# First h from raw x, DMA transposes and 3.5-chunk q and S in a fused linear-attention and gated-MLP kernel

## The chip, the cores and the metric

The kernel runs on one NeuronCore of a Trainium2 chip. Times are device microseconds (us) of whole executions. A single profiled execution of each kernel gives the span, the engines' busy times and the waits; the span is 1.7 to 2.3 us shorter than the time of the same run. PE is TensorE's matmul stream, PEld its weight loads, DVE VectorE, ACT ScalarE, POOL GpSimd, and SP the engine whose queue issues nearly all DMAs ("SPq" in the profile). PSUM is the memory that TensorE writes; the kernel uses eight parts of it, called banks.

## The reference

Token count 2048, width 448 (3.5 times 128), hidden width 1792, 16 heads of 28. All arrays are bfloat16.

```python
xn = layernorm(x)                       # over the last axis, eps 1e-5
q, k, v = split_heads(xn @ wqkv)        # linear attention: no softmax
pq, pk = phi(q), phi(k)                 # where(t > 0, t + 1, exp(t)) + 1e-6
kv, z = sum_s pk[s] v[s], sum_s pk[s]
o = (pq @ kv) / (pq @ z + 1e-6)
s = o @ wo
h = relu(xn @ w1 + b1) ** 2             # 1792 columns
g = silu(h @ w2 + b2)
return x + s * g
```

## The kernel before

All work is recorded as operations with estimated durations. PE and SP run them in the order in which they are written; a small list scheduler chooses the order on DVE, ACT and POOL from those estimates, and the order is then fixed. Tokens come in 16 tiles of 128, handled as four groups of four tiles.

```python
def pe_transpose(tiles):                 # xn -> xT, on PE, through one PSUM bank
    ... last = e.transpose(v[:, o : o + P], xn[:, si, c * P : (c + 1) * P], ident[:, :])
    ... # evicted (copied out of PSUM) by DVE (0.69 us for two tiles) or ACT

def pe_four(a, b, c, d):                 # four output tiles, all matmuls on 64 rows;
    ...                                  # the two halves of the array run side by side
for g in range(NG):                      # groups of four token tiles
    if g == 0:
        pe_transpose([1]); pe_two(kk(0), kk(1), False)
        pe_transpose([2, 3]); pe_two(kk(2), kk(3), True)
    if g + 1 < NG:
        ln(4 * g + 4, 4 * g + 8)         # statistics, rstd, normalise, copy of columns 384..447
    ...                                  # K, q and h of this group, in groups of four
    pe_transpose([4 * g + 4, 4 * g + 5])
    pe_transpose([4 * g + 6, 4 * g + 7])
    ...
# then token sums (xn^T pk), folds (these sums times the v weights, then times wo), den (pq @ z),
# spreads (1/den repeated over a head's columns), gate tiles gg(si) = h[si] @ w2 and S tiles ss(si)
```

The width of 448 leaves a half chunk of 64 rows. The kernel before copies columns 384 to 447 of xn a second time, so that the transposed half chunk lies on both halves of the partitions, and runs h, K and q in 64-row halves that pack without loss. q and S use four chunks of 112 columns (four heads each). A "gate tile" below is 14 matmuls of 448 columns; h is 14 output tiles a group.

## Time and profile before

158.31 us median of two runs (157.43 and 159.19); span of the profile 157.6 us.

| what | value | where it is read |
|---|---|---|
| PE busy | 148.4 of 157.6 us | page, busy times |
| useful PE work begins, h begins, PE ends | 7.5, 14.6, 153.7 us | timeline |
| tail after PE's last matmul | 3.9 us | timeline |
| transposes on PE | 16 matmuls in about 1.0 us, four groups | timeline |

The page of the kernel before: busy times with their share of the span, then the span in 40 equal slices, where 9 means busy at least 90% and PEclk is the clock granted to TensorE in tenths.

```profile
PE 148.4 (94%) x1131; PEld 76.5 (49%) x1131; DVE 105.9 (67%) x237; ACT 70.8 (45%) x129; POOL 35.4 (22%) x49
PE   5969999999999869999999999999999999999990
PEclk9999999999999987999999999999999999999999
```

PE is the bound, with small dents in slices 2 and 13 to 14 (counted from 0). After the second dent the clock is lower (8 and 7). The waits of PE, kernel before: engine and line that waited, what released it, us in total, times, longest.

```profile
PE pb L463 <- DVE xn L449: 2.2, 2, 1.9
PE pb L564 <- DVE xT L473: 0.8, 1, 0.8
```

The timeline of PE around that dent, kernel before: start, us, engine, line, operation, tiles, shapes, count, and in brackets the idle time before it.

```profile
52.37 1.03 PE L597 MATMUL pb<-xT,w 64*128 64x512 bf16 x8
...
56.63 1.07 PE L463 MATMUL pb<-ident,xn 128*128 128x128 bf16 x16 [1.94 <-DVE xn L449]
57.63 1.70 PE L585 MATMUL pb<-xT,w_qkv 64*112 64x512 bf16 x8
59.12 1.91 PE L597 MATMUL pb<-xT,w 64*128 64x512 bf16 x8
```

Eight h matmuls take 1.03 us at 52.4 us and 1.91 us at 59.1 us: after 1.94 us of waiting and 1.0 us of transposes the clock was halved for about 3.4 us. This happens in some executions only: of 40 runs of this kernel taken later, those with a mean granted clock of 0.984 to 0.988 took 158.8 to 160.0 us, those with 0.994 to 1.0 took 157.2 to 158.2. The 1.6 us between them is what this stretch costs.

### The profile page before, as it was taken

To read this page: it belongs to the slowest core of one execution; us is meant where nothing else is said; L and a number is where in the kernel's file an instruction comes from. 1 tells how busy PE (TensorE), PEld (TensorE's weight loads), DVE (VectorE), ACT (ScalarE), POOL (GpSimd) and SP (SyncE) were. 2 spreads that over 40 slices of the span, in tenths; PEclk is the share of its full clock that TensorE was granted. 3 is DMA by queue.
4 is the path that set the end of the run, shared out by engine and by line. 5 is a ranking of instruction groups with operands and counts; after the bars stand their busy time and mean duration, and the time that the engine had idled before them with its cause. 6 is when DMAs were issued, how large, how long until landed. Compare 5 with 4: busy or idle time off the path is not lost.

```text
span 157.6 us, 2827 instructions
## 1 busy us (share of the span) xinstructions
PE 148.4 (94%) x1131; PEld 76.5 (49%) x1131; DVE 105.9 (67%) x237; ACT 70.8 (45%) x129; POOL 35.4 (22%) x49
## 2 busy tenths in 40 slices
PE   5969999999999869999999999999999999999990
PEld 5834545455444444445454454444555555555540
DVE  0879896789995992969998056799633444433373
ACT  3442688768787752877811269512211112211110
POOL 7502500055001630007300000000022522233252
PEclk9999999999999987999999999999999999999999
DMA  4999991000000000000000000000001110001013
GB/s 130 324 402 296 347 294 38 0 2 0 4 0 0 4 0 0 0 4 0 2 0 4 0 0 2 4 0 0 0 0 50 41 58 29 29 29 33 29 55 120
DMA packets 7721, 9.19 MB, mean 58 GB/s; under 512 B 604, under 2 KB 6812, under 8 KB 7708
## 3 DMA queue, kind: packets, MB, share of 16 engines
q1 hardware_dynamic: 7148, 8.55, 17.7%
q10 hardware_dynamic: 560, 0.46, 0.9%
q8 instruction: 9, 0.15, 0.4%
q14 instruction: 4, 0.03, 0.1%
HBM read 7.17 MB, written 1.84 MB: 57 GB/s over the span
## 4 chain that ended last, share of the span: by engine, by line
PE 86%; DVE 6%; DMA 3%; SPq 2%; ACT 1%; issue 0%; DVEq 0%
PE pb L755 27%; PE pb L597 25%; PE pb L783 8%; PE pb L585 7%; PE pb L564 6%; PE pb L626 6%; DMA b1r<-in_B_b_dram 3%; PE pb L463 3%; DVE xn L421 2%; SPq L365 2%; DVE pk L554 1%; PE pb L632 1%; DVE pk L547 1%; PE pb L734 1%; DVE xT L473 1%; DVE xn L449 1%
## 5 line engine op out<-in xcount | busy, mean ns | idle before, releaser
L597 PE MATMUL pb<-xT,w 64*128 64x512 bf16 x392 | 48.2, 381 | 0.0
L755 PE MATMUL pb<-w,r 128*128 128x448 bf16 x224 | 44.9, 353 | 0.0
L606 ACT ACTIVATE r<-pb,b1f 128x512 bf16<-128x512 f32 x56 | 34.9, 691 | 8.3 <-PE pb L597 8.3
L755 PEld LDWEIGHTS pb<-w,r 128*128 128x128 bf16 x224 | 21.6, 98 | 20.7 <-issue 0.9
L597 PEld LDWEIGHTS pb<-xT,w 64*128 64x128 bf16 x392 | 19.0, 95 | 22.6 <-issue 1.4
L797 POOL TENSOR_TENSOR obuf<-obuf,x_tok 128x448 bf16<-128x448 bf16 x14 | 14.3, 1032 | 63.9 <-DVE obuf L792 63.9
L772 ACT ACTIVATE gbuf<-gbuf 128x448 bf16<-128x448 bf16 x16 | 9.2, 577 | 41.9 <-DVE gbuf L764 41.9
L764 DVE TENSOR_TENSOR gbuf<-pb,b2b 128x448 bf16<-128x448 f32 x16 | 10.0, 625 | 23.5 <-PE pb L755 23.1
L612 DVE TENSOR_TENSOR r<-r 128x512 bf16<-128x512 bf16 x56 | 20.6, 433 | 7.5 <-ACT r L606 7.5
L575 POOL TENSOR_TENSOR zacc<-zacc,pk 128x448 f32<-128x448 f32 x13 | 13.7, 1055 | 46.8 <-DVE pk L554 45.4
L585 PE MATMUL pb<-xT,w_qkv 64*112 64x512 bf16 x112 | 15.7, 395 | 0.0
L564 PE MATMUL pb<-w_qkv,xT 64*128 64x448 bf16 (+1 forms) x100 | 12.8, 350 | 1.3 <-DVE xT L473 0.8
L783 PE MATMUL pb<-msb,pqT 112*128 112x448 bf16 x64 | 13.9, 352 | 0.0
L542 ACT ACTIVATE pqT<-pb 112x512 bf16<-112x512 f32 x16 | 8.7, 594 | 10.3 <-PE pb L585 10.3
L401 DVE BATCH_NORM_STATS2 st<-x_tok 128x6 f32<-128x448 bf16 x16 | 9.4, 613 | 4.3 <-DMA x_tok<-in_A_x_dram 4.3
L792 DVE TENSOR_TENSOR obuf<-pb,gbuf 128x448 bf16<-128x448 f32 x16 | 10.0, 625 | 2.1
L554 DVE SCALAR_TENSOR_TENSOR pqT<-pb,pqT 112x512 bf16<-112x512 f32 x16 | 10.9, 688 | 0.3
L585 PEld LDWEIGHTS pb<-xT,w_qkv 64*112 64x112 bf16 x112 | 7.5, 133 | 5.9 <-issue 1.3
L542 ACT ACTIVATE pk<-pb 128x448 bf16<-128x448 f32 x16 | 7.8, 540 | 5.1 <-PE pb L564 5.1
L547 DVE TENSOR_SCALAR pk<-pk 128x448 bf16<-128x448 bf16 x16 | 6.8, 432 | 4.6 <-ACT pk L542 4.6
L742 DVE TENSOR_TENSOR pqT<-pqT,pb 112x512 bf16<-112x512 bf16 x16 | 9.9, 680 | 0.0
L554 DVE SCALAR_TENSOR_TENSOR pk<-pb,pk 128x448 bf16<-128x448 f32 x16 | 9.6, 619 | 0.3
(60 smaller groups left out, 100.8 us busy)
## 6 DMA issues: line engine op xcount, KB each, us to landing
out_dram<-obuf SPq DMA_DIRECT2D x16, 112.0 KB, 1.7
w<-in_B_w_dram SPq DMA_DIRECT2D x1, 1568.0 KB, 16.2
x_tok<-in_A_x_dram SPq DMA_DIRECT2D x3, 448.0 KB, 9.4
w<-in_B_w_dram SPq DMA_DIRECT2D x1, 1344.0 KB, 8.2
w_qkv<-in_A_wqkv_dram SPq DMA_DIRECT2D x2, 336.0 KB, 7.9
x_tok<-in_A_x_dram SPq DMA_DIRECT2D x2, 224.0 KB, 3.7
w<-in_B_w_dram SPq DMA_DIRECT2D x2, 224.0 KB, 8.9
w_o<-in_A_wo_dram SPq DMA_DIRECT2D x1, 392.0 KB, 17.3
```

The source lines that it names most:

```text
L542: "act", lambda e, _: e.activation(out=slot, in_=ps(buf)[0:rows, 0:n], func=AF.Exp), [buf, "actw"],
L554: lambda e, _: e.scalar_tensor_tensor(out=slot, in0=ps(buf)[0:rows, 0:n], scalar=1.0 + 1e-6, in1=slot, op0=ALU.add, op1=ALU.max),
L564: return e.matmul(ps(b)[:, 0:D], xT[rows, c, si * P : (si + 1) * P], w_qkv[rows, c, D : 2 * D], start=start, stop=stop)
L575: lambda e, _: e.tensor_tensor(out=o[:, :], in0=pk[:, 0, :] if i == 1 else zacc[:, :], in1=pk[:, i, :], op=ALU.add),
L585: return e.matmul(ps(b)[0:PD, 0:512], w_qkv[rows, c, m * PD : (m + 1) * PD], xT[rows, c, g * 512 : (g + 1) * 512], start=start, stop=stop,)
L597: return e.matmul(ps(b)[:, 0:512], w_1[rows, c, fi * P : (fi + 1) * P], xT[rows, c, g * 512 : (g + 1) * 512], start=start, stop=stop,)
L606: lambda e, _: e.activation(out=slot, in_=ps(b)[:, 0:512], func=AF.Relu, bias=b1f[:, fi : fi + 1]),
L612: "dve", lambda e, _: e.tensor_tensor(out=slot, in0=slot, in1=slot, op=ALU.mult), [("r2", g, fi)],
L755: last = e.matmul(ps(b)[:, 0:D], r2[:, fi, si * P : (si + 1) * P], w_2[:, fi, :], start=(fi == 0), stop=(fi == NF - 1),)
L764: "dve", lambda e, _: e.tensor_tensor(out=gs, in0=ps(b)[:, 0:D], in1=b2b[:, :], op=ALU.add),
L783: last = e.matmul(ps(b)[:, 0:D], pqT[0:PD, c, si * P : (si + 1) * P], msb[0:PD, c, 0:D], start=(c == 0), stop=(c == 3),)
L797: return e.tensor_tensor(out=ob, in0=ob, in1=x_tok[:, si, :], op=ALU.add)
```

## The change

It aims at PE: begin h before the statistics of x are known, and take the transposes off PE.

- **Raw-x head.** Group 0's h comes from x^T without normalisation. `xn @ w1 + b1 = rstd * (x @ w1 - mean * colsum(w1) + sdev * b1)`, so each h tile gets one more matmul with five rows (mean and sdev in split precision, column sums and b1), and rstd squared is applied to the gate tile. The column sums cost 70 small matmuls.
- **DMA transposes.** The normalised x is transposed by DMA, two transposes a token tile: all columns, and columns 320 to 447 again for the upper half rows.
- **3.5 chunks.** q and S use chunks of 128 and one half chunk of 64, paired over two token tiles.
- **Early gate tiles.** Gate tiles 0 to 3 run among groups 1 and 2. The last gate and S tiles are split to shorten the tail.

The core of the diff, cut:

```diff
+        def x_transpose(lo, hi):
+            for k in range(lo, hi):
+                add("sp", lambda e, _, k=k: e.dma_start_transpose(xT[:, k, 0:4, :], xn[:, k, :]),
+                    [("xn", k), "xn_pad"], [("xT", k)], 0.5, nbytes=P * 512 * 3)
+                add("sp", lambda e, _, k=k: e.dma_start_transpose(xT[:, k, 4:5, :], xn[:, k, 320:448]),
+                    [("xn", k)], [("xTu", k)], 0.5, nbytes=P * P * 3)
...
+        warm(36)
+        raw_transpose(0)
+        col_sums(0)
+        pe_four(*(H0[i] for i in range(4)), close=False, part=0, need=xa[0])
+        raw_transpose(2)
...
+        row_transpose()
+        aug([H0[i] for i in range(4)], range(4), True)
+        for si in (0, 2):
+            for k in (si, si + 1):
+                ln_norm(k)
+            x_transpose(si, si + 2)
+        pe_two(H0[5], H0[7], close=False)
...
+        load_x(8, 12)
+        ln(4, 8)
...
-            pe_transpose([4 * g + 4, 4 * g + 5])
-            pe_transpose([4 * g + 6, 4 * g + 7])
...
+                for si in ...: for c in range(3):        # S: six full-height matmuls for two tiles,
+                    e.matmul(..., pqT[:, c, ...], msb[:, c, :], start=(c == 0), stop=False)
+                for o, b in enumerate(bufs):               # then two on 64 rows each
+                    e.matmul(ps(b)[:, 0:D], pqx[r, u, j, :], msb[r, 3, :], start=False, stop=True)
```

The 0.5 in `x_transpose` is the scheduler's own idea of what issuing one costs the queue.

## The prediction

> **What bounds the kernel now.** The page: PE is busy 148.4 of 157.6 us (94%), DVE 105.9, ACT 70.8. The chain of waits is 86% PE. The matmul stream runs at its pace nearly everywhere: gate tiles are 14 matmuls of 448 columns in 2.65 us, h is 62 half-row matmuls in 6.69 us (108 ns each). So only less PE work or fewer PE holes can help. From the timeline I add the useful PE work at steady pace: h 42.3, gate 42.4, S 12.2, q 12.1, token sums 10.8, K 10.6, transposes 4.0, rest about 5: 139 us. It occupies 7.5 to 153.8 us, so about 7 us are lost: about 2.4 between 7.5 and 13.6 (transpose, copy, K, in turn), 2.2 us of PE waiting for the normalised x before the third transposes, and about 1.7 after it at half speed (8 matmuls in 1.63 us at 57.7). Before 7.5 us nothing useful runs; h starts at 14.6. The tail after PE's last matmul is 3.8 us.
>
> **Removed.** 48 of 64 PE transposes (62 ns each in groups of 16): 3 us net of the raw ones kept (20). q on 3.5 chunks: 12.1 to 10.8. S: 12.2 to 10.7. About 5.7 us of DVE/ACT transpose evictions and the twin copies.
> **Added on PE.** 70 small column-sum matmuls (40-60 ns each by analogy with the 60 ns of the 112-column fold matmuls): 3-4 us; the 5-row matmul in four row tiles 0.9; row transposes 0.3; kv-by-wo 4 to 8 matmuls 0.5; small z and bias work 0.4. Net PE work: about 139 before, 138.5-139 after. Arithmetic is therefore a wash; the gain must come from the start and from the holes.
> **Moved.** First h no longer needs statistics: it needs raw x (landed 3.9 us in the trace), the first quarter of w1 and the b1 row. At 300-400 GB/s (DMA row of the page) these land by 6-7 us, so useful work starts at about 6.8 instead of 7.5-9, and then runs without the transpose-copy-K ping-pong. K and q of group 0 start near 22.7 us, group 1's K near 27. Early gate tiles give PE work while DVE catches up.
>
> **DMA transposes.** 32 of them, issued in order from one queue behind the loads (about 11.5 us). The Trainium skill, "VectorE: DVE Perf Modes", section "The three transpose paths", gives 1309 ns for one 128x128 by this path; the trace of before has none, so no measurement. My estimate from it: about 1.5 us per token tile (two transposes), 4 tiles by about 19.5, 8 by about 26.5: just in time. At 2.5 us per tile PE would stall 3-5 us around 25-33 us.
>
> **Sum.** Start 6.8 + work 138.7 + remaining holes 3 (two or so from DVE near 100% at 25-50 us, one when the first two spreads need four banks each in quick succession) = 148.5; tail 3.8 (gate tile 15's silu and two split outputs: unchanged); span 152.3; runs exceed the span by 0.7: **153.0 us**, range 149.5 to 156.5. Faster by over 2%: 0.77; within 2%: 0.19; slower: 0.04.
>
> **What would show it.** Right: first h matmul by 8 us; PE busy about 147 with few waits; no PE wait on the DMA transposes; the 2.2 us wait and the slow clock at 57 us gone; PE's last matmul near 148.5. Wrong: PE waits on xT at K0 or K1 (transposes over 2 us per tile); PE at half speed in 5-10 us because only 36 warm-up matmuls precede the short transposes; column sums over 60 ns each; PE waiting for banks in the spreads; gate tile 0 waiting for w2, which is queued behind the transposes; strided xT reads making h slower than 108 ns.

## The result

175.67 us median (175.52 to 175.81, two runs), correct, against 158.31: the ratio of the fast runs is 1.1106 (95% interval 1.095 to 1.126). A ratio here and below is the mean time of one kernel's fast runs over that of the kernel before in the same rounds, so it isn't quite the ratio of the medians quoted.

The page of the changed kernel, busy times and slices:

```profile
PE 154.3 (89%) x1155; PEld 73.4 (42%) x1155; DVE 93.5 (54%) x229; ACT 76.5 (44%) x146; POOL 35.7 (21%) x55
PE   6798969339999962999999999999999999999990
PEclk9999999965999996599999999999999999999998
```

There are two large holes, near 26 to 37 us and 62 to 68 us, and a slow clock after each. PE is busy for 5.9 us more than before, and most of that is no added work: part of it runs at half speed (e3_four below, with the same matmuls, is busy for 148.9 us). The waits of PE, changed kernel:

```profile
PE pb L670 <- DMA xT<-xn: 8.5, 2, 4.3
...
PE pb L590 <- DMA xT<-xn: 3.4, 3, 1.8
```

11.9 us of waits, all for the DMA transposes. The timeline of the SP queue, changed kernel; here the second column is the time that the queue was occupied with issuing:

```profile
14.20 1.31 SPq L501 DMA_TRANSPOSE xT<-xn  x1
15.55 1.22 SPq L505 DMA_TRANSPOSE xT<-xn  x1
...
25.35 0.59 SPq L413 DMA_DIRECT2D x_tok<-in_A_x_dram  x1
...
35.01 1.24 SPq L505 DMA_TRANSPOSE xT<-xn  x1
...
56.72 1.23 SPq L501 DMA_TRANSPOSE xT<-xn  x1
```

The same trace asked for the tile xT: duration in ns (least, median, most), first and last start.

```profile
L501 SPq DMA_TRANSPOSE xT<-xn x16: 1212/1264/2034, 14.2 to 74.9; - x16
L505 SPq DMA_TRANSPOSE xT<-xn x16: 1222/1232/1243, 15.6 to 76.2; - x16
```

L501 moves 512 columns and L505 moves 128, and they occupy the queue for 1.26 and 1.23 us (medians; the longest takes 2.03 us). A token tile takes 2.5 us, a group 10 us. The eight tiles of groups 0 and 1 keep the queue busy from 14.2 to 36.3 us. A load of x stands between them and is issued at 25.35 us. The third group's transposes start only at 56.7 us, because its normalisation comes that late in DVE's order. The issue list of the same profile gives the median time from issue to landing, in us:

```profile
xT<-xn SPq DMA_TRANSPOSE x32, 2.5
```

The timeline of PE, changed kernel:

```profile
7.96 0.50 PE L664 MATMUL pb<-xr,w 64*128 64x256 bf16 x6
...
32.23 0.93 PE L590 MATMUL pb<-w_qkv,xT 64*128 64x448 bf16 x8 [1.17 <-DMA xT<-xn]
37.44 1.46 PE L670 MATMUL pb<-xT,w 64*128 64x512 bf16 x6 [4.28 <-DMA xT<-xn]
...
42.99 0.83 PE L670 MATMUL pb<-xT,w 64*128 64x512 bf16 x6
...
68.31 1.46 PE L670 MATMUL pb<-xT,w 64*128 64x512 bf16 x6 [4.23 <-DMA xT<-xn]
```

The first h matmul runs at 7.96 us, as hoped. But after each wait of more than 4 us the same six h matmuls take 1.46 us instead of 0.83. The Trainium skill, "TensorE: Matmul & The Clock Gate", section "HAM oscillation — how this bites in real kernels", warns of PE gaps above about 3.4 us, after which the clock is halved; this trace agrees: about 3 us into each of these two waits, of 4.28 and 4.23 us, the granted clock fell to 0.5, for 6.8 us. Two of the experiments show a halved clock after shorter waits (last section).

### Where PE's time went

I summed the time from each matmul's start to the next one's start, at most its own duration, by the part of the kernel that issued it; what is left, from PE's first warm-up matmul at 1.6 us on and without the warm-up itself, is idle time. This is worked out from the profiles and counts a slow clock as work. All in us, for the kernel before, the changed one and the experiments below.

| part | before | changed | e4_pe | e3_four | x_both | b1_before_dma |
|---|---|---|---|---|---|---|
| head: column sums, 5-row matmul, raw and row transposes | 0 | 5.9 | 6.6 | 6.3 | 5.9 | 0 |
| transposes of xn on PE | 4.4 | 0 | 3.8 | 0 | 0 | 1.4 |
| h | 43.8 | 47.3 | 44.4 | 44.5 | 43.9 | 43.0 |
| K | 11.0 | 13.9 | 11.2 | 11.1 | 10.6 | 11.0 |
| q | 13.2 | 11.5 | 11.5 | 11.5 | 11.7 | 12.2 |
| S | 12.3 | 12.2 | 12.2 | 12.2 | 11.6 | 12.3 |
| gate | 42.8 | 43.4 | 43.2 | 43.4 | 43.4 | 42.8 |
| token sums, folds, den, rest | 15.2 | 16.2 | 16.2 | 16.2 | 16.2 | 15.2 |
| sum | 142.7 | 150.5 | 149.0 | 145.1 | 143.2 | 137.8 |
| idle | 3.7 | 13.9 | 2.3 | 1.5 | 1.4 | 4.9 |

### The profile page after: what moved, and what is told of

The parts are those of the page before. It is cut to its first block, busy times and chain, and to the rows that moved or that the text cites. A ratio compares the mean times of both kernels' runs of the same rounds, so it can differ in the third digit from the quotient of the medians.

```text
span 174.0 us, 2943 instructions
## 1 busy us (share of the span) xinstructions
PE 154.3 (89%) x1155; PEld 73.4 (42%) x1155; DVE 93.5 (54%) x229; ACT 76.5 (44%) x146; POOL 35.7 (21%) x55
## 3 DMA queue, kind: packets, MB, share of 16 engines
q1 hardware_dynamic: 20238, 10.95, 24.6%
## 4 chain that ended last, share of the span: by engine, by line
PE 83%; DVE 6%; DMA 5%; SPq 1%; issue 1%; ACT 1%; POOL 0%; DVEq 0%; POOLq 0%
PE pb L1019 25%; PE pb L670 25%; PE pb L834 5%; PE pb L590 5%; PE pb L1068 5%; PE pb L612 4%; DMA xT<-xn 3%; PE pb L1146 2%; DMA x_tok<-in_A_x_dram 2%; PE pb L664 2%; PE pb L627 1%; DVE pk L578 1%; PE pb L1073 1%; PE pb L920 1%; PE pb L840 1%
## 5 line engine op out<-in xcount | busy, mean ns | idle before, releaser
L670 PE MATMUL pb<-xT,w 64*128 64x512 bf16 (+1 forms) x234 | 34.9, 402 | 8.9 <-DMA xT<-xn 8.5
L642 ACT ACTIVATE r<-pb,b1f 128x512 bf16<-128x512 f32 x42 | 25.8, 688 | 7.3 <-PE pb L670 7.3
L670 PEld LDWEIGHTS pb<-xT,w 64*128 64x128 bf16 (+1 forms) x234 | 12.4, 99 | 25.9 <-issue 8.4
L590 PE MATMUL pb<-w_qkv,xT 64*128 64x448 bf16 (+1 forms) x106 | 17.1, 407 | 3.4 <-DMA xT<-xn 3.4
L590 PEld LDWEIGHTS pb<-w_qkv,xT 64*128 64x128 bf16 (+1 forms) x106 | 6.6, 108 | 12.0 <-DMA xT<-xn 4.4
L612 PE MATMUL pb<-xT,w_qkv 64*128 64x512 bf16 (+1 forms) x78 | 11.1, 377 | 0.0
L639 ACT ACTIVATE r<-pb 128x512 bf16<-128x512 f32 x14 | 7.3, 597 | 5.7 <-PE pb L815 5.7
L648 ACT ACTIVATE r<-r 128x512 bf16<-128x512 bf16 x16 | 9.5, 632 | 0.0
L834 PE MATMUL pb<-pk,xn 128*128 128x448 bf16 x48 | 9.4, 353 | 0.0
L1068 PE MATMUL pb<-msb,pqT 128*128 128x448 bf16 x42 | 9.1, 353 | 0.0
```

The source lines that it names most:

```text
L590: return e.matmul(ps(b)[:, 0:D], xT[rw, si, chunk(rw, c), :], w_qkv[rw, c, D : 2 * D], start=start, stop=stop)
L612: return e.matmul(ps(b)[:, 0:512], w_qkv[rw, c, m * P : (m + 1) * P], xT[rw, 4 * g : 4 * g + 4, chunk(rw, c), :], start=start, stop=stop,)
L642: rl = lambda e, _: e.activation(out=slot, in_=ps(b)[:, 0:512], func=AF.Relu, bias=b1f[:, fi : fi + 1])
L648: return e.activation(out=slot, in_=slot, func=AF.Square)
L670: return e.matmul(ps(b)[:, 0:512], lhs, rhs, start=start, stop=stop)
L834: last = e.matmul(ps(b)[:, 0:D], xn[:, si, c * P : (c + 1) * P], pk[:, si, :], start=(si == 0), stop=(si == NT - 1),)
```

## The experiments

Theory A: issuing a DMA transpose costs the SP queue about 1.25 us whatever its size, and 32 of them in order starve PE; the slow clock follows. Rivals: the transfer itself is the bound (B); or the order of the norms on DVE is the loss (C). A second question is whether the rest of the change gains anything.

### e1_order: tell the scheduler the true issue cost

```diff
-    [("xn", k), "xn_pad"], [("xT", k)], 0.5, nbytes=P * 512 * 3,
+    [("xn", k), "xn_pad"], [("xT", k)], 1.25, nbytes=P * 512 * 3,
```

(and likewise for the second transpose.)

> Only the scheduler's own figure for issuing one DMA transpose goes from 0.5 to 1.25 us, the value the trace of the changed kernel shows; the same 32 transposes, but the normalisation of the third and fourth groups moves far ahead in DVE's order. Theory A (the queue's 1.25 us per transpose, 2.5 us per token tile, is the bound where PE waits): the waits at 25 to 38 us stay (about 7 us idle plus slow clock), the one at 63 to 70 us (4.7 us idle plus about 2.4 us of slow clock) goes: 167 to 169 us. Rival C (the order of the norms is the whole loss): below 161 us.

166.91 us (165.61 to 167.31), ratio 1.0524. The waits of PE, e1_order:

```profile
PE pb L670 <- DMA xT<-xn: 3.9, 1, 3.9
PE pb L590 <- DMA xT<-xn: 1.7, 1, 1.7
```

The third group's transposes start at 41.3 instead of 56.7 us and PE's second wait is gone; the first stays. So half of the regression, about 9 us, goes with the right figure in the scheduler's table, and half stays with the queue itself. The two aren't separate losses: e2_twin and e3_four keep the 0.5 and hardly wait. Rival C is not the whole loss.

### e2_twin: one transpose a token tile

```diff
-    add("sp", ... dma_start_transpose(xT[:, k, 4:5, :], xn[:, k, 320:448]) ...)
+    add("dve", ... tensor_copy(xn[:, lo:hi, 448:512], xn[:, lo:hi, 384:448]) ...)
```

(the 0.5 stays.)

> The second transpose of each token tile is dropped: the 64 spare columns of the normalised x are a DVE copy of its last 64, as in the kernel before, so 16 transposes instead of 32, each of 512 columns. Theory A (fixed issue cost of about 1.25 us per transpose whatever its size): a group's transposes take 5 us of the queue instead of 10, most PE waits go, 160 to 165 us. Rival B (the crossbar transfer is the bound, in proportion to columns: 512 instead of 640): a fifth off, 171 to 173 us.

158.46 us (158.23 to 158.86), ratio 1.0007. Half of the instructions, four fifths of the columns, and 17 us less. Rival B falls. The gain was larger than I expected, as both waits depend on the same queue; PE's only wait for a transpose is 1.2 us.

### e3_four: one transpose for four token tiles

```diff
-    for k in range(lo, hi): add("sp", ... dma_start_transpose(xT[:, k, 0:4, :], xn[:, k, :]) ...)
+    add("sp", ... dma_start_transpose(xT[:, lo:hi, :, :] as 128 x 16 x 128, xn[:, lo:hi, :] as 128 x 2048) ...)
-    def ln(lo, hi, stats=True, step=2):
+    def ln(lo, hi, stats=True, step=4):
```

> As e2_twin, and one transpose instruction moves four token tiles: 4 instructions instead of 32. Theory A with a fixed cost per instruction: issue stays near 1.3 us for 2048 columns, no PE wait on transposes beyond their latency, 154 to 160 us. Rival B (cost follows the columns): the issue or the landing grows about fourfold to 5 us or more and the time is that of e2_twin, or worse because nothing can start before the whole group has landed.

157.10 us (156.90 to 157.41), ratio 0.9918. The SP queue, e3_four:

```profile
13.53 2.12 SPq L504 DMA_TRANSPOSE xT<-xn  x1
...
23.12 1.86 SPq L504 DMA_TRANSPOSE xT<-xn  x1
```

its issue list, and the durations of all four transposes:

```profile
xT<-xn SPq DMA_TRANSPOSE x4, 4.4
L504 SPq DMA_TRANSPOSE xT<-xn x4: 1862/2024/2711, 13.5 to 54.6; - x4
```

Sixteen times the columns of L505 cost 1.9 to 2.7 us of the queue instead of 1.23, and landing takes 4.4 us instead of 2.5. The cost is mostly fixed per instruction, though not as fixed as the 1.3 us that I expected. PE no longer waits for a transpose at all. The two edits of form together (e2_twin and this one) take the changed kernel from 175.7 to 157.1 us; PE's idle time falls by 12.4 us and its work by 5.4 us (table), the slow clock.

### e4_pe: PE transposes instead, the rest of the change kept

```diff
-    x_transpose(si, si + step)
+    pe_transpose(0); pe_transpose(2)      # before h tiles 12 and 13 of group 0; later groups likewise
```

> All DMA transposes undone: PE transposes with the twin copy and an eviction of 0.69 us per two tiles, as before; the raw-x head, the 3.5 chunks and the early gate tiles stay. If the DMA transposes are the whole cause of the regression: 151 to 155 us, the value predicted for the change. If the rest of the change costs time as well (column sums, 5-row matmul, pairs of 64-row matmuls, other order): 156 us or more.

161.74 us (161.15 to 161.98), ratio 1.0206. I had thought of 151 to 155. With the transposes back on PE (3.8 us) the change is slower than the kernel before. The DMA transposes had hidden that the rest of the change is no gain. The table shows where: 6.6 us of head, and S, which was to shrink by 1.5 us, did not.

### e5_quads and e6_ss4: 64-row matmuls between full-height ones

In e3_four's chain of waits a pair of h tiles (six full-height matmuls and two on 64 rows) stands beside a group of four in 64-row halves only:

```profile
12.70 1.72 PE pb L672 x8
...
18.33 3.13 PE pb L672 x28
```

The group of four is shown with its change from and to other forms; within a run of fours it takes 3.02 us. The pair has the array time of seven 512-column matmuls, since its two halves may run side by side; at 0.216 us each (3.02 us over 14) that is 1.51 us, and it takes 1.72. e5_quads turns six of eight pairs into fours:

```diff
-    pe_two(H0[4], H0[6], close=False) ... pe_two(H0[5], H0[7], close=False)
+    pe_four(*(H0[i] for i in range(4, 8)), close=False)
-    quads("H1.8 H1.9 H1.10 H1.11"); quads("H1.12 H1.13")
+    quads("H1.9 H1.12 H1.11 H1.13")          # the others go with q tiles; K and q pairs likewise
```

> Base e3_four. Six of the eight pairs that run six full-height matmuls and then two 64-row ones (1.72 us a pair in the trace of e3_four) become parts of groups of four in 64-row halves only (3.02 us per four, 0.755 a unit). Theory S (each change between full-height and 64-row matmuls costs PE about 0.1 us, so a pair loses 0.2): the h, K and q groups shrink by 1.1 to 1.3 us in sum, and the time with them: 155.7 to 156.2. Rival (the pairs are slow because of the weights they read or of waits on buffers): no change, 157 us.

155.50 us (155.24 to 156.28), ratio 0.9838, against 0.9918 for e3_four, each against the kernel before in its own rounds: 0.8%, or 1.3 us. The intervals of these ratios overlap, as the two kinds of runs of the kernel before widen both; the runs themselves don't (155.24 to 156.28 against 156.90 to 157.41). h and K shrink by 1.0 us, q and the small terms move by 0.1.

e6_ss4 computes S in fours: twelve full-height matmuls, then four on 64 rows.

```diff
-    ss(0, False) ... ss(1, False) ...        # two token tiles each
+    ss(0, 4) ... ss(4, 4) ... ss(8, 4)       # four token tiles each
```

> Base e3_four. S in batches of four token tiles instead of two for tiles 0 to 11: the same 42 full and 14 half-height matmuls, but the 64-row ones stand in three rows of four instead of six rows of two. Theory S: three switches there and back fewer, 0.6 us less on PE, time 156.3 to 156.7. Rival (the 64-row matmuls of S simply cost 0.15 us each wherever they stand): no change within 0.3 us.

156.24 us (155.85 to 156.76), ratio 0.9877: 0.4%, or 0.65 us, better than e3_four. The timeline of PE in e3_four and then in e6_ss4:

```profile
140.28 1.30 PE L1069 MATMUL pb<-msb,pqT 128*128 128x448 bf16 x6
141.51 0.36 PE L1074 MATMUL pb<-msb,pqx 64*128 64x448 bf16 x2
141.81 2.82 PE L1020 MATMUL pb<-w,r 128*128 128x448 bf16 x14
```

```profile
139.48 2.43 PE L1067 MATMUL pb<-msb,pqT 128*128 128x448 bf16 x12
141.84 0.55 PE L1073 MATMUL pb<-msb,pqx 64*128 64x448 bf16 x4
142.33 2.82 PE L1020 MATMUL pb<-w,r 128*128 128x448 bf16 x14
```

From first start to the gate tile's start: 1.53 us for two tiles, 2.85 us for four, instead of 3.06. Both results agree with about 0.2 us lost for each excursion from full-height matmuls to 64-row ones and back. The Trainium skill, "TensorE: Matmul & The Clock Gate", section "The mechanism", says that a weight load overlaps running matmuls only when its row group differs. A 64-row load behind a full-height matmul shares rows with it, which would fit; but full-height loads do overlap full-height matmuls here (0.189 us each), which that sentence doesn't allow. The trace of e3_four shows where the 0.2 us lie: in the full-height S matmuls each weight load begins with the matmul before its own, 0.189 us ahead, but at each change of form the first loads begin together with their own matmuls. The first 64-row matmul starts 0.285 us after the last full-height one, and the next full-height one 0.292 us after the second 64-row one: 0.10 us late each time, as long as one load (0.093 to 0.098 us). Why the load isn't started ahead there is not shown.

### x_both and e7_lategates

x_both has both edits.

> e5_quads and e6_ss4 together: if both effects are of PE time and PE bounds the kernel, their gains add: 1.7 to 1.9 us below e3_four, about 155.3 us.

155.06 us (154.61 to 155.65), ratio 0.9799 (0.9746 to 0.9853). The gains add, as they do where PE bounds.

e7_lategates takes x_both and moves the four early gate tiles back:

```diff
-    gg(0) ... gg(1) ... gg(2) ... gg(3)      # among groups 1 and 2
+    for si in range(4): ggs(si)              # after fold_wo
```

> Base x_both (155.1 us, PE idle 1.4 us). The four early gate tiles go back behind fold_wo. Theory G (they fill PE while DVE clears its backlog of phi, squares and norms): PE waits of 1 to 3 us appear between 25 and 75 us, 156 to 158 us. Rival (they are only moved work, PE would not wait without them): within 0.5 us of x_both.

154.99 us (154.62 to 155.66), ratio 0.9797. No difference in time, but not for the rival's reason alone. One wait as theory G expected it does appear, for the fourth group's transpose (0.4 us in x_both):

```profile
PE pb L592 <- DMA xT<-xn: 1.5, 1, 1.5
```

PE's idle time grows by 0.8 us and the gate's own sum shrinks by 0.5, with fewer changes of form. On balance the early gate tiles are worth nothing.

### b1_before_dma: the kernel before with the mended transposes alone

```diff
-    pe_transpose([4 * g + 4, 4 * g + 5]); pe_transpose([4 * g + 6, 4 * g + 7])
+    x_transpose(4 * g + 4, 4 * g + 8)        # one instruction, right after ln(); xT tile-major
```

> The kernel before with one part of the change alone, in the mended form: the PE transposes of groups 2 to 4 become one DMA transpose of four token tiles each; no raw-x head, no 3.5 chunks, no early gate tiles. Theory W (apart from the transposes the change is a wash or worse on PE: the head costs about 7 us of PE work and buys about 6 us of earlier start): 3.3 us of PE transposes, the 2.2 us wait and the slow clock after it go, 152 to 154 us, better than e3_four. Rival (the raw-x head and the rest carry a gain of their own that the transposes hid): 156 us or more, not better than e3_four.

154.45 us (154.02 to 154.86), ratio 0.9759 (0.9709 to 0.981). The lowest median of all, with some twenty changed lines, just above the 152 to 154 us expected; its interval overlaps those of x_both and e9_nofold_lead below. Its page and its waits of PE:

```profile
PE 142.6 (93%) x1083; PEld 73.2 (48%) x1083; DVE 104.3 (68%) x233; ACT 68.8 (45%) x127; POOL 35.6 (23%) x49
```

```profile
PE pb L575 <- DMA xT<-xn: 1.5, 1, 1.5
PE pb L463 <- DVE xn L449: 1.0, 1, 1.0
```

PE's work falls by 4.9 us (table): 3.0 of transposes, the rest the slow clock, in h and q. The long wait for the normalised x is gone. There was no slow stretch in its six runs, while the kernel before had it in five of its eleven runs of the same rounds. Against the other six (157.19 to 157.68 us) the gain is 3.0 us, as much as the removed transposes took. The three long transposes occupy the queue for 2.6 to 3.0 us here, more than in e3_four; why isn't shown:

```profile
L485 SPq DMA_TRANSPOSE xT<-xn x3: 2626/2806/2985, 24.2 to 42.1; - x3
```

b2_lead tried to remove the remaining 1.5 us wait:

```diff
-    op.late = late - op.dur - LAT ...
+    op.late = late - op.dur - LAT - (3.0 if op.nbytes and op.reads else 0.0) ...
```

> Base b1_before_dma (154.5 us, PE waits 1.5 us for the DMA transpose of the second group). The scheduler takes 3 us more lead for the norms that feed a DMA transpose. If that wait is on the path: it goes, 152.5 to 153.5 us. If the moved norms push phi back instead, PE waits elsewhere and the time stays at 154 to 155 us.

154.46 us (154.03 to 155.44), ratio 0.9761: nothing gained. The transpose is issued at 23.5 instead of 24.2 us and PE still waits 1.5 us for it.

### e8_nofold and e9_nofold_lead: the change without the raw-x head

```diff
-    raw_transpose(0); col_sums(0); pe_four(*H0...); ... aug(...)      # h of group 0 from raw x
+    pe_transpose([0]); pe_transpose([1]); K0.0 K0.1; pe_transpose([2, 3]); K0.2 K0.3; ...   # as before
```

> Base x_both, without the raw-x head: group 0 is normalised and transposed on PE as in the kernel before, K and q of group 0 first, h with b1 as bias; 3.5 chunks, DMA transposes of groups 1 to 3 in fours and early gate tiles stay. Theory W (the raw-x head is a wash: column sums, 5-row matmul, raw and row transposes are 5.8 us of PE against 1.4 us of transposes and a start hole of 2.5 to 4 us): 154 to 156 us. Rival (starting h from raw x is worth 2 us or more): over 157 us.

160.84 us (160.36 to 164.05, of which one slow run is left out of the ratio), ratio 1.0147. This looks like a verdict for the head, and isn't: my new order put K of the second group before its transpose had landed. The waits of PE, e8_nofold:

```profile
PE pb L626 <- DMA xT<-xn: 5.7, 1, 5.7
```

A slow clock followed. So e9_nofold_lead moves those K tiles behind all h tiles of group 0, gives the norms more lead as in b2_lead, and puts the transposes into the scheduler's table at 2.0 us instead of 0.5 (b1_before_dma has 2.0 too):

```diff
-    "... Q0.2 H0.9 K1.0 H0.11 H0.12 K1.1 H0.13 K1.2"
+    "... Q0.2 H0.9 H0.11 H0.13 H0.12 K1.0 K1.1 K1.2"
```

> Base e8_nofold, whose 5.7 us wait for the second group's DMA transpose (and the slow clock after it) spoiled the comparison: its K tiles now come after all h of the first group, and the scheduler takes 3 us more lead for norms that feed a DMA transpose. Theory W (the raw-x head is a wash): wait gone or under 1 us, 153.5 to 155.5 us, within 1.5 us of x_both. Rival (starting h from raw x is worth 2 us or more): over 157 us although that wait is gone.

154.87 us (154.55 to 156.72), ratio 0.9766. The waits of PE in its profiled run, which was its slowest, at a granted clock of 0.989:

```profile
PE pb L684 <- DMA xT<-xn: 2.1, 1, 2.1
PE pb L503 <- DVE xn L519: 1.7, 1, 1.7
```

Within 0.2 us of x_both by the median, and that with a wait of 2.1 us left, where I had asked for 1 us or less. The raw-x head buys nothing: it starts h some 7 us earlier (7.3 us in x_both, 14.8 here) and pays about 6 us of PE work for it, against 1.4 us of transposes and the holes of the old start.

## Why the prediction was wrong

- **The bound and the start: right.** PE bounds the kernel; the first h matmul ran at 7.96 us; the head itself had waits of 1 us or less, and no slow clock.
- **"About 1.5 us per token tile (two transposes)": wrong, and the cause of the miss.** Measured: 2.5 us (medians 1.26 and 1.23). I had taken 1309 ns for a 128x128 transpose from the skill's table of transpose paths and put two of them at 1.5 us, as if they overlapped on the queue; no trace stood behind that. The trace shows 1.23 us of queue time even for 128 columns, and only 1.9 to 2.7 us for 2048 (e3_four). e2_twin and e3_four show it by experiment: 16 instructions fewer take off 17 us, 28 fewer 18.6 us.
- **"At 2.5 us per tile PE would stall 3-5 us": the case was named, and its size was wrong.** The waits came to 11.9 us, with 5.4 us of slow clock on top. The sum left out a second stall at the third group (e1_order: about 9 us in all, from a 0.5 in the scheduler's table) and the halved clock after waits of more than 4 us.
- **"Net PE work: about 139 before, 138.5-139 after": wrong by about 6 us for the change.** e3_four, with hardly a wait and no slow clock, shows 145.1. About 2 us of this were missed in the kernel before already: by the same measure it takes 142.7 us, 1.7 of them its slow stretch, so about 141 and not 139. The change then adds about 4 us where I had a wash. The column sums were cheaper than said (2.1 us, not 3 to 4), the 5-row matmul cost 1.3 rather than 0.9, and the 20 raw transposes 2.1 to 2.5 instead of about 1. h cost 44.5 instead of 42.3, S stayed at 12.2 instead of 10.7, q fell to 11.5 instead of 10.8, and the gate took 43.4 instead of 42.4 (42.8 in the kernel before). e5_quads and e6_ss4 show that 1.9 us of this are changes between full-height and 64-row matmuls, which I had counted as free.
- **"K and q of group 0 near 22.7, K of group 1 near 27": too early.** PE finished h of group 0 at 24.6 us; K of group 1 began at 32.2.
- **"The 2.2 us wait and the slow clock at 57 us gone": right for the mended forms only.** In the changed kernel larger waits took their place.
- **"Early gate tiles give PE work while DVE catches up": worth nothing on balance.** e7_lategates is level. DVE was expected near 100% at 25 to 50 us; in the changed kernel it was starved there (53% busy), in e3_four it was 91% busy and PE hardly waited.
- **Tail unchanged: about right** (4.2 us against 3.9). "Runs exceed the span by 0.7" was not: one span was compared with the median of two unlike runs, and every run whose span is on record exceeds it by 1.7 us or more.

So two steps failed. The cost of a DMA transpose explains 18.6 us of the 22.7 us between 153.0 and 175.7; the remaining 4.1 us, and the absence of a gain in e4_pe, are mostly PE work that I took to be a wash: 145.1 against 138.7 in e3_four, partly made up by a start 1.4 us earlier and holes 1.5 us smaller than in the sum. What stays open is why a weight load isn't started ahead at a change of form, and why a transpose of 2048 columns holds the queue for 1.9 us in one place and up to 4.4 in another (e9_nofold_lead).

## What to carry to other kernels

Count DMA transposes by what they cost the queue that issues them, not by bytes: one transpose of four tiles at 2 to 3 us beats eight at 10 us, and an issue cost that a scheduler or a model believes to be 0.5 us and is 1.25 us can cost as much again through the order it chooses. Work moved off a bound engine is a gain only if its replacement arrives in time, as a long wait can be charged again through a halved clock (5.4 us here). And a saving of matmul columns must be weighed with the changes of form that it brings: 3.5 chunks instead of 4 saved an eighth of the columns of S and no time until the half chunks were batched.

## What the Trainium skill lacked or had wrong

- "DMA: Bandwidth & Descriptors", section "DMA Transpose (X-bar)": no page gives the cost of issuing a DMA transpose for trn2 by name; the nearest is a table on that page, about trn3, with cycle counts for unnamed earlier generations. Here it is 1.23 us of the queue for 128 columns, 1.26 for 512 (medians) and 1.8 to 4.4 for 2048 over the experiments (median 2.0 in e3_four, 2.8 in b1_before_dma; 128 rows, SBUF to SBUF), with 2.4 to 2.5 us to landing for up to 512 columns and 4.4 us for 2048 (medians). The page's general rule to coalesce small transfers would have helped; it isn't said of transposes, nor in time of the issuing queue.
- "VectorE: DVE Perf Modes", section "The three transpose paths": 1309 ns for 128x128 by DMA is near the issue time seen here, but reads as a cost for that size; four times the columns cost the queue 0.03 us more, and landing took 2.4 us.
- "TensorE: Matmul & The Clock Gate", sections on the clock gate: they name an idle window of about 3.4 us. In the kernel before, 1.94 us of waiting followed by 1.0 us of transposes was enough in some executions (granted clock 0.984 to 0.988, 1.6 us lost) and not in others. The page's remark that transposes don't count as busy in the same way, in the section "Part 4: PE-mode transpose", would fit that case, but transposes aren't needed: in e9_nofold_lead the clock was halved for 3.4 us after a wait of 2.1 us at 26.2 us, with PE's last transposes at 11.1 us, and in e1_order after a wait of 1.7 us. Nor does the length of the wait decide alone: 1.8 us in the changed kernel (at 24.7 us) and 1.5 us in b1_before_dma were followed by a full clock.
- The same page, section "The mechanism": nothing on the cost of going from full-height matmuls to 64-row ones and back; another page, "TensorEngine Tiling (Array Packing)", section "Key Properties", says that changing the tiling mode drains TensorE, without a figure. Here it was about 0.2 us there and back (e5_quads, e6_ss4). The sentence that a weight load overlaps only when the row group differs doesn't hold for the full-height loads here (gate tiles at 0.189 us a matmul).
